# Weight pieces moved from ahead of the expert gathers to behind them, and idle matmuls between the first expert's transposes

## The chip, the cores and the metric

One core of a Trainium2 chip runs the whole program. The metric is the device time of one execution in microseconds; a kernel's time is the median of its executions. Each execution has a state: "slow" when it is over 1.5% above the fastest of the same kernel. A ratio between two kernels is the mean time of one kernel's fast runs over that of the other's fast runs of the same rounds, so it is not quite the ratio of the medians quoted beside it.

## The reference

Attention over 8 batches of 8 heads (576 x 64, block-causal in blocks of 64), then a mixture of 8 experts with the expert of each row given. Cut to the core:

```python
attn_out = _attn_ref(q, k, v)                       # 8 x 8 x 576 x 64
x = attn_out.transpose(0, 2, 1, 3).reshape(4608, 512)
for e in range(8):                                  # w1[e]: 512 x 1024, w2[e]: 1024 x 512
    mask = domain_id == e
    h = np.maximum(x[mask] @ w1[e], 0.0)
    out[mask] = h @ w2[e]
```

## The kernel before

Attention is worked off in 32 pairs of heads. TensorE computes, ScalarE takes the exps, VectorE scales, and each batch's rows x are stored to a buffer in DRAM (`x_rows`). After the last pair GpSimd gathers the rows of each expert from there, five blocks of 128 rows, by an indirect DMA. TensorE transposes a block, runs a first product (relu on ScalarE) and a second product, and GpSimd scatters the result.

The weights of experts 0 to 3 are fetched during the last twelve pairs, in 32 pieces (8 an expert), by the same GpSimd queue that later gathers. `loads(p)` runs once a step:

```python
        if p == 4 * B - 12:
            cast_v(fn, B - 1)
            for e in range(4):
                wts.extend(load_expert(e))          # 8 pieces an expert
        if p >= 4 * B - 12:                         # 13 steps, p = 20 .. 32
            for f in wts[:2]:
                f()
            del wts[:2]
```

So 26 pieces go out ahead of the first gather and 6 behind the first ten. After attention:

```python
    ps = aps.tile([128, 2, 512], F32, name="ps", tag="ps", bufs=2)
    for i in range(36):                             # idle matmuls
        nc.tensor.matmul(out=ps[:, i % 2], lhsT=identh[:], rhs=w1s[0][:, 0, 0:512], ...)
    # ... cut ...
    def gather(tok):
        g = msb.tile([128, NB, DM], F16, name="xg", tag="xg", bufs=3)
        for blk in range(NB):
            nc.gpsimd.indirect_dma_start(out=g[:, blk, :], out_offset=None, in_=xd,
                in_offset=bass.IndirectOffsetOnAxis(ap=tok[:, 1, blk : blk + 1], axis=0), ...)
        return g
    # ... cut ...
    xgs = {e: gather(tok_of(e)) for e in range(2)}
    for f in wts:                                   # the pieces that are left
        f()
    for e in range(E):
        if e + 2 < E:
            xgs[e + 2] = gather(tok_of(e + 2))      # behind those pieces
        # ... first product of e; the second one transposes the rows of e + 1 between its blocks
```

Expert 2's rows are first touched when expert 1's second product begins.

## Time and profile before

| | us |
|---|---|
| time of the kernel before, median of 3 (range) | 333.39 (332.84 to 333.70) |
| the profiled execution | 325.94 (span 323.5, clock 0.950) |
| attention's end (last x) in it | 145.5 |
| first gather / first transposes / first product of expert 0 | 152.7 / 155.9 / 159.5 |
| second product of expert 0 / 1 / 2 starts | 172.5 / 190.9 / 209.3 |

The lines of the page are in the prediction.

### The profile page before, as it was taken

The numbers are of one execution on the slowest core, as the hardware profiler recorded it, in microseconds if no ns is written. First come the engines' busy times: TensorE is split into PE (matmuls) and PEld (weight loads), VectorE is DVE, ScalarE is ACT, GpSimd is POOL, SyncE is SP. The second block draws the span as 40 slices with busy tenths as digits, with TensorE's granted clock in tenths as the row PEclk, the third lists the DMA queues.
The fourth block names the chain that finished last, engine by engine and source line by source line (L and its number), as shares of the span: only waits on it lengthen the run. The fifth ranks groups of instructions, "written<-read, shape, count | busy, mean of one in ns | idle before, by whom it ended". The sixth has DMA issues, their size and how long they took to land. (4 is left out here: it accounts for less than half of the span.)

```text
span 323.5 us, 8592 instructions
## 1 busy us (share of the span) xinstructions
PE 272.4 (84%) x3658; PEld 176.6 (55%) x3658; DVE 154.0 (48%) x298; ACT 146.6 (45%) x208; POOL 205.4 (63%) x274
## 2 busy tenths in 40 slices
PE   2588697978877999777599999999999999999930
PEld 1366565746655766553255665756566565756510
DVE  2868789799857887740103514041322405042220
ACT  5558575758757988750053240605133150604200
POOL 8668989998894833301786648777777876133230
PEclk9999899879979999999589999999999999999995
DMA  7999799998998599995359327979799896112030
GB/s 159 201 220 193 161 267 188 247 211 187 228 200 199 130 208 232 212 235 137 97 126 225 140 83 145 242 187 227 217 198 228 172 229 207 49 65 81 33 118 0
DMA packets 36472, 55.68 MB, mean 172 GB/s; under 512 B 9838, under 2 KB 22638, under 8 KB 36432
## 3 DMA queue, kind: packets, MB, share of 16 engines
q0 software_dynamic: 26128, 49.17, 70.7%
q1 hardware_dynamic: 9776, 5.81, 6.6%
q8 instruction: 30, 0.49, 0.6%
q10 hardware_dynamic: 528, 0.13, 0.2%
q14 instruction: 10, 0.08, 0.1%
HBM read 67.15 MB, written 15.20 MB: 255 GB/s over the span
## 5 line engine op out<-in xcount | busy, mean ns | idle before, releaser
L352 ACT ACTIVATE A<-ps 128x1024 f16<-128x1024 f32 (+1 forms) x96 | 83.2, 883 | 41.0 <-PE ps L347 27.5
L565 ACT ACTIVATE hT<-ph 128x640 f16<-128x640 f32 (+1 forms) x72 | 46.4, 645 | 113.6 <-PE ph L559 94.6
L583 POOL DMA_INDIRECT out_dram<-osb,tok x40 | 40.6, 1014 | 45.5 <-DVE osb L582 35.6
L540 DVE COPY xT<-pt 128x512 f16<-128x512 f16 x40 | 16.9, 425 | 103.2 <-PE pt L537 103.2
L559 PE MATMUL ph<-xT,w1h 128*128 128x320 f16 x384 | 56.4, 307 | 1.1 <-DVE xT L540 1.1
L527 POOL DMA_INDIRECT xg<-x_rows,tok x40 | 40.6, 1015 | 26.0 <-PE ps L515 14.1
L576 PE MATMUL po<-w2h,hT 128*128 128x512 f16 x240 | 56.7, 379 | 0.0
L78 POOL DMA_DIRECT2D vst<-in_v_dram x56 | 42.8, 787 | 14.0 <-DMA kh<-in_k_dram 5.9
L559 PEld LDWEIGHTS <-w1h 128*128 128x128 f16 x384 | 38.5, 100 | 18.9 <-issue 1.4
L339 DVE COPY QK<-PT 128x576 f16<-128x576 f16 x64 | 45.5, 750 | 3.3 <-PE PT L335 3.1
L576 PEld LDWEIGHTS <-hT 128*128 128x128 f16 x320 | 29.9, 98 | 29.3
L347 PE MATMUL ps<-QK 64*128 64x512 f16 (+3 forms) x256 | 37.2, 328 | 5.0 <-issue 2.3
L403 PE MATMUL po<-vS,A 128*128 128x65 f16 x640 | 36.9, 200 | 4.0 <-issue 4.0
L582 DVE COPY osb<-po 128x512 f32<-128x512 f32 x40 | 27.4, 684 | 18.8 <-PE po L576 18.8
L398 PE MATMUL po<-VE,ATE 128*128 128x130 f16 x160 | 33.0, 232 | 3.9 <-DVE x L420 3.1
L403 PEld LDWEIGHTS <-A 128*128 128x128 f16 x640 | 32.1, 102 | 6.6 <-issue 6.5
L420 DVE TENSOR_TENSOR x<-po,rc 128x768 f16<-128x768 f32 x32 | 30.6, 958 | 1.1
L335 PE MATMUL PT<-identh,kh 64*64 64x64 f16 x576 | 16.8, 201 | 8.1 <-DVE inv L234 3.0
L398 PEld LDWEIGHTS <-ATE 128*128 128x128 f16 x160 | 16.0, 100 | 11.9 <-issue 9.7
L537 PE MATMUL pt<-identh,xg 128*128 128x128 f16 x160 | 15.9, 225 | 5.1 <-issue 3.9
L335 PE MATMUL PT<-identh,qh 64*64 64x64 f16 x576 | 16.6, 203 | 4.3 <-DVE QK L339 3.3
L335 PEld LDWEIGHTS <-qh 64*64 64x64 f16 x576 | 13.5, 116 | 12.3 <-issue 10.0
(88 smaller groups left out, 271.8 us busy)
## 6 DMA issues: line engine op xcount, KB each, us to landing
vst<-in_v_dram POOLq DMA_DIRECT2D x63, 128.0 KB, 6.9
w1h<-in_moe_w_dram POOLq DMA_DIRECT2D x24, 256.0 KB, 7.1
w2h<-in_moe_w_dram POOLq DMA_DIRECT2D x24, 256.0 KB, 10.4
vst<-in_moe_w_dram POOLq DMA_DIRECT2D x16, 256.0 KB, 7.4
qh<-in_q_dram POOLq DMA_DIRECT2D x14, 288.0 KB, 6.6
kh<-in_k_dram POOLq DMA_DIRECT2D x14, 288.0 KB, 9.4
x_rows<-x SPq DMA_DIRECT2D x7, 512.0 KB, 10.6
vst<-in_v_dram SPq DMA_DIRECT2D x4, 256.0 KB, 5.6
```

Of the source, the lines that this page charges most:

```text
L78: eng.dma_start(out=vst[b % 3][:, 0:4, n], in_=v[b, n, 0:512, :].rearrange("(c p) d -> p c d", p=128))
L335: nc.tensor.transpose(out=PT[h, j], in_=src[h, hp, 64 * j : 64 * j + 64], identity=identh[h, h])
L339: nc.vector.tensor_copy(out=QK[:, s].rearrange("p (n j) -> p n j", j=9), in_=PT[:].rearrange("p j n -> p n j"))
L347: nc.tensor.matmul(out=o[:, i], lhsT=QK[h, 1, 128 * c : 128 * c + 128], rhs=QK[h, 0, 64 + 128 * c : S], start=True, stop=True)
L352: nc.scalar.activation(out=o, in_=i, func=AF.Exp, scale=0.125)
L398: nc.tensor.matmul(out=o[:, 1:131], lhsT=st["AE"][:, 128 * m : 128 * m + 128], rhs=VE[b % 2][:, m, hp, 1:131], start=True, stop=(m == 0))
L403: nc.tensor.matmul(out=o[:, 1 + 65 * i : 66 + 65 * i], lhsT=at_block(st, i, c, m), rhs=vS[b % 3][:, c, hp, 1 + 65 * i : 66 + 65 * i], star ...
L527: nc.gpsimd.indirect_dma_start(out=g[:, blk, :], out_offset=None, in_=xd, in_offset=bass.IndirectOffsetOnAxis(ap=tok[:, 1, blk : blk + 1], ...
L559: nc.tensor.matmul(out=ph[:, i, 0:hw], lhsT=w1_cols(w1h, dc, fc), rhs=xT[:, dc, hw * i : hw * i + hw], start=(dc == 0), stop=(dc == 3))
L565: nc.scalar.activation(out=hT[:, fc].rearrange("p (i n) -> p i n", i=2)[:, i0:i1], in_=ph[:, i0:i1, 0:hw], func=AF.Relu)
L576: nc.tensor.matmul(out=po[:], lhsT=hT[:, fc, 128 * blk : 128 * blk + 128], rhs=w2h[:, fc, :], start=(fc == 0), stop=(fc == 7))
L583: nc.gpsimd.indirect_dma_start(out=dst[blk], out_offset=bass.IndirectOffsetOnAxis(ap=tok[:, 0, blk : blk + 1], axis=0), in_=osb[:], in_off ...
```

## The change

The intent is to leave the DMA engines to the last stores of x, so that the gathers start sooner, and to keep TensorE's clock up while the first blocks arrive (it was 0.66 from 152.00 to 159.46 us in the profile before). Ten pieces go out ahead of the gathers (one in each of ten steps) and 22 behind the first ten gathers; the 36 idle matmuls write another buffer; five more follow each of expert 0's first two transposed blocks.

```diff
-        if p >= 4 * B - 12:
-            for f in wts[:2]:
+        if 4 * B - 12 <= p < 4 * B - 2:
+            for f in wts[:1]:
                 f()
-            del wts[:2]
+            del wts[:1]
...
-    ps = aps.tile([128, 2, 512], F32, name="ps", tag="ps", bufs=2)
-    for i in range(36):
-        nc.tensor.matmul(out=ps[:, i % 2], lhsT=identh[:], rhs=w1s[0][:, 0, 0:512],
-                         start=True, stop=True)
+    def warm(t, n):
+        for i in range(n):
+            nc.tensor.matmul(out=t[:], lhsT=identh[:], rhs=w1s[0][:, 0, 0:512],
+                             start=True, stop=True)
+
+    warm(aps.tile([128, 512], F32, name="PT", tag="PT", bufs=2), 36)
...
                     transpose_block(xgs[0], xT, blk)
+                    if blk < 2:
+                        warm(mps.tile([128, 512], F32, name="po", tag="po", bufs=2), 5)
```

## The prediction

> **What bounds the kernel now.** I read the page first (busy slices, clock, DMA), then the busy table cut at the borders of the stages, then the timelines of GpSimd and TensorE around the seam between attention and the experts, and last the landing times of the gathers. The chain that ended last holds only the final scatter and is no help.
>
> ```profile
> PEclk9999899879979999999589999999999999999995
> DMA  7999799998998599995359327979799896112030
> ```
>
> DMA is full through the late attention steps, nearly empty for a few slices at the seam, and busy again in the experts. The clock has one deep dip, at the seam. By stage (columns: us, busy us of PE, PEld, DVE, ACT, POOL with counts, clock, DMA share, GB/s):
>
> ```profile
> 107.81:144.02 36.21, 30.84 (x777) 22.60 (x774) 25.70 (x43) 29.45 (x42) 13.85 (x27) 1.00 1.08 217
> 144.02:152.00 7.98, 7.98 (x43) 3.48 (x39) 1.19 (x2) 0.00 (x0) 0.00 (x0) 1.00 0.83 183
> 152.00:159.46 7.46, 1.81 (x13) 1.14 (x13) 1.27 (x3) 0.00 (x0) 5.25 (x6) 0.66 0.25 70
> 159.46:172.21 12.75, 12.12 (x71) 7.45 (x71) 0.76 (x2) 6.22 (x15) 10.62 (x14) 0.80 0.63 132
> 172.21:190.86 18.65, 18.65 (x128) 11.47 (x126) 6.59 (x20) 5.71 (x9) 12.63 (x13) 1.00 0.55 164
> 190.86:310.20 119.34, 119.34 (x786) 71.62 (x784) 33.99 (x64) 34.50 (x49) 72.30 (x87) 1.00 0.67 160
> ```
>
> From 172.21 on TensorE never idles: whatever moves the start of that stretch moves the end by as much, as long as no new wait opens in it. The seam is the only weak place: 152.00 to 159.46 holds 1.81 us of PE work, and 159.46 to 172.21 runs at clock 0.80.
>
> ```profile
> 114.91 0.54 POOL L120 DMA_DIRECT2D w1h<-in_moe_w_dram  x1 [2.82 <-DMA w1h<-in_moe_w_dram]
> 116.15 0.53 POOL L120 DMA_DIRECT2D w1h<-in_moe_w_dram  x1 [0.70 <-DMA w1h<-in_moe_w_dram]
> ...
> 123.79 0.53 POOL L123 DMA_DIRECT2D w2h<-in_moe_w_dram  x1 [0.84 <-DMA w2h<-in_moe_w_dram]
> ...
> 152.69 1.10 POOL L527 DMA_INDIRECT xg<-x_rows,tok  x1 [14.11 <-PE ps L515]
> ...
> 165.56 1.18 POOL L120 DMA_DIRECT2D vst<-in_moe_w_dram  x2
> 166.68 2.18 POOL L123 DMA_DIRECT2D vst<-in_moe_w_dram  x4
> 169.16 1.07 POOL L527 DMA_INDIRECT xg<-x_rows,tok  x1 [0.30 <-issue]
> ```
>
> GpSimd's timeline. Eight weight pieces are in flight at most; each further one waits for the piece eight before it. So the issue times show the rate: 114.91 to 123.79 is seven pieces, 1.27 us each. The first gather (152.69) is put down to the idle matmuls, but in the built program it waits for the last attention matmul and for the stores of x_rows; the idle matmuls come after the counter value it asks for. In the completion records of the trace the last store lands at 151.74, so that store is the gate, and the gather follows 0.95 us later.
>
> ```profile
> 144.07 7.93 PE L515 MATMUL ps<-w1h,identh 128*128 128x512 f16 x36
> ...
> 145.53 0.41 ACTq L436 DMA_DIRECT2D x_rows<-x  x1
> ...
> 155.88 0.59 PE L537 MATMUL pt<-identh,xg 128*128 128x128 f16 x4 [3.88 <-issue]
> ...
> 159.46 7.14 PE L559 MATMUL ph<-xT,w1h 128*128 128x320 f16 x32 [0.52 <-DVE xT L540]
> ...
> 190.91 0.39 PE L537 MATMUL pt<-identh,xg 128*128 128x128 f16 x4
> ```
>
> The timeline of all engines: the last store, issued at 145.53, takes 6.2 us because weight pieces share the DMA engines with it. The last line is the first touch of expert 2's gathered rows (xg), at the start of the second matrix product of expert 1.
>
> ```profile
> DMA to landing us min/median/max: 2.7/3.6/7.8
> ```
>
> The gathers' landing times. The 7.8 is the gather issued at 169.16, right behind six pieces: it lands at 176.95, after the last piece (176.61), and the next four at 0.3 to 1.0 us steps.
>
> [...] A piece reads 128x1024 fp32, 524 KB; in 1.27 us that is 413 GB/s[...]. [...] Here it was 0.5 from 154.33 to 164.57[...], and came back 5.1 us after the dense matmuls began at 159.46.
>
> **The change part by part.** First, pieces. There are 32 (four experts of eight). Before, 26 are issued ahead of the first gather and 6 after the tenth. Now 10 are ahead and 22 after it. "A step" paces nothing on the chip: these loads go to fresh buffers, so GpSimd issues ten as fast as eight in flight allow, and they land by about 127 (the tenth landed at 126.88 before). Attention is not touched: it is held by ScalarE's exps, 29.45 of 36.21 us busy, and by PE at 30.84.
>
> The stores of x_rows are then alone. The store issued at 106.62 and 107.11, which had no weights beside it, landed 3.7 us after its second issue, at 576 rows. The last two stores, about the same number of rows each, should be done at about 148.3, so the first gather starts at 148.3 + 0.95 = 149.3, 3.4 us sooner. Its block lands 2.9 us later as now (152.69 to 155.58), 152.2, just as the 36 idle matmuls end (152.0). Moving them from ps to PT takes off a wait for the last exps but nothing visible: they started 0.05 us behind attention's last matmul.
>
> Second, the idle matmuls between transposes. Blocks land 1.3 us apart; four transposes take about 0.4 us, so five matmuls of 0.216 us (7.93/36 gives 0.22) nearly fill the gap and keep the clock. Warm, the third block is transposed by 155.8, its copy and handover of 0.5 us lead to 156.3, the first half of expert 0's first product costs 32 x 0.134 = 4.3 us instead of 7.1, the two further transposes 1.2 us, the second half 4.6 us: 166.4, where the kernel before is at 172.46. This part with the earlier gather is worth 6.0 us at this point.
>
> Third, what is paid. TensorE goes on: second product 9.75 us (172.46 to 182.21), expert 1's first product 8.7 us: 166.4 + 18.5 = 184.9 when it wants expert 2's rows. Their gather stands behind the 22 pieces in GpSimd's order and in the ring. Ten gathers take 12.87 us of issue (152.69 to 165.56), so the first piece goes out at 162.2. The first piece after the gathers landed 4.28 us after its issue (169.84), now 166.5; 21 more at 1.27 us make 193.2. The rows follow 0.34 us behind (as 176.95 behind 176.61), and TensorE starts 0.27 us later (155.58 to 155.85): 193.8, against 190.91 before. So the lead of 6.0 us becomes a wait of 8.9 us and a lag of 2.9 us.
>
> In a wait that long the clock surely falls. Dense work after it is slow for about as long as before, 5.1 us, and half of that is lost: 2.6 us. Sum: -6.0 + 8.9 + 2.6 = +5.5 us, 338.9 us. The pieces of expert 1 (needed from 176.1, landing from 166.5 to 172.9) and of expert 2 (by 183.1) make nobody wait. Later GpSimd runs some 9 us behind at first, but the gather of expert 4 landed 13 us before its use and expert 4's weights over 20 us, so I see no second wait; nor room to win anything back on a TensorE that is busy throughout.
>
> **The rivals.** (a) The intent comes true: rows of expert 2 are in time, and the 6 us are kept: 327 to 328. For it: the same bytes are moved, and DMA stood at 0.25 to 0.63 between 152 and 172. Against it: 16 more pieces are 20.3 us, and the old gather of expert 2 had only 190.91 - 176.95 = 14.0 us to spare; the 3.4 us of earlier start don't make up the rest. (b) The wait opens but the seam's clock matters little and DMA is a little faster than I count (1.25 us a piece, stores done at 147): wait ends at 192, cold loss 1.7: 336. (c) Stores end later[...]: gather at 150.5, cold loss 3.4: 341. (d) The filler matmuls themselves delay a cold TensorE: at half clock five take 2.2 us in a gap of 0.7 us. It costs up to 3 us at the seam, but disappears in the later wait, as does any gain there. The end depends on the DMA chain alone.
>
> **Range and chances.** The sum is the start of the gather (148.3 to 150.5), the rate of pieces (1.25 to 1.30, times 21 is 1 us) and the cold loss (1.7 to 3.4). Together 335.5 to 342.0. Two per cent slower is 340.06, inside the upper part: 0.28. Two per cent faster is 326.7, beyond even (a): 0.03. Within: 0.69.
>
> **What would show it.** Right: first gather near 149; clock 1.0 through 152 to 166; a PE gap of 7 to 10 us ahead of the transposes of expert 2's rows (released by the DMA of xg), with a clock of 0.5 after it; DMA full from 165 to 193. Wrong: no such gap, or gathers landing ahead of pieces issued before them, or pieces quicker than 1.2 us; then (a). If the gather still starts near 152, the stores were not slowed by the weights.

"Here it was 0.5 from 154.33 to 164.57" speaks of TensorE's clock. That the clock would fall in the later wait too, and that work behind it would again be slow for 5.1 us, was my estimate from this one dip; the range of 1.7 to 3.4 us for the cold loss was assumed.

## The result, and the profile after

The changed kernel took 347.02 us (median of 4, 342.77 to 348.16) beside 333.54 us (median of 4) for the kernel before; the ratio of fast runs is 1.0324, 95% interval 1.0232 to 1.0415. It is slower, and by more than the predicted range allowed. The profiled execution took 348.07 us and is a slow one; its readings are checked below against fast runs.

The clock and DMA rows of the changed kernel's page (40 slices each):

```profile
PEclk9999868787999999999899986999999999999985
DMA  8999899989981990223799947959899595202020
```

DMA, which was full up to about 150 us before, now stands at 0 to 0.3 in slices 16 to 19 (about 130 to 164 us) and is full in slices 21 to 23 (173 to 199 us): the pieces have moved there. The clock's deep dip (slices 20 and 21 before) is gone; there is a slight one left in slice 20 and a new one in slices 24 and 25, 199 to 216 us. By stage, cut at the changed kernel's own borders (columns as in the prediction: us, busy us and count of PE, PEld, DVE, ACT, POOL, then clock, DMA share, GB/s):

```profile
159.86:175.68 15.82, 12.02 (x72) 7.37 (x72) 0.85 (x2) 6.37 (x15) 11.31 (x17) 0.89 0.69 142
175.68:194.29 18.61, 18.61 (x126) 11.21 (x123) 6.69 (x20) 5.43 (x9) 8.92 (x14) 1.00 1.12 209
194.29:198.69 4.40, 0.00 (x1) 0.00 (x1) 0.00 (x0) 0.70 (x1) 3.26 (x4) 1.00 1.00 282
198.69:226.00 27.31, 22.65 (x125) 12.52 (x126) 5.11 (x10) 4.93 (x7) 21.05 (x26) 0.81 0.76 178
```

TensorE is busy without a gap from 175.68 to 194.29, does nothing for 4.40 us while DMA runs full, and then needs 27.31 us for work that took 18.4 before. The next lines are TensorE's timeline in that last stretch (the brackets: idle time before, and what ended it):

```profile
198.69 0.52 PE L539 MATMUL pt<-identh,xg 128*128 128x128 f16 x4 [4.40 <-DMA xg<-x_rows,tok]
...
206.23 0.39 PE L539 MATMUL pt<-identh,xg 128*128 128x128 f16 x4
210.98 3.57 PE L578 MATMUL po<-w2h,hT 128*128 128x512 f16 x8 [4.36 <-issue]
```

The first line is the predicted wait for expert 2's rows. GpSimd's timeline says why they are late: the last piece (`vst`) is issued and, only then, the gather.

```profile
188.51 0.53 POOL L123 DMA_DIRECT2D vst<-in_moe_w_dram  x1 [0.69 <-DMA w2h<-in_moe_w_dram]
189.74 1.06 POOL L529 DMA_INDIRECT xg<-x_rows,tok  x1 [0.70 <-DMA vst<-in_moe_w_dram]
```

The third line of TensorE's timeline above was not predicted. VectorE's timeline has its counterpart:

```profile
209.90 0.42 DVE L542 COPY xT<-pt 128x512 f16<-128x512 f16 x1 [6.12 <-remote]
...
214.20 0.42 DVE L542 COPY xT<-pt 128x512 f16<-128x512 f16 x1 [3.28 <-remote]
```

The transposes that these copies wait for end by 204.67 and 206.62 on TensorE; the copies start 5.23 and, counting from the time when VectorE was free, 3.28 us late. TensorE then runs out of buffers, stands still for 4.36 us, and its clock falls a second time (0.5 from 209.07 to 215.90). I call this a late handover: the producer has ended, the consumer is free, and yet it starts late. The trace's semaphore records place the delay: the count that the two copies wait for rises at 209.88 and 214.18, 0.02 us ahead of them, and not when the transposes end. So it is in 107 of the 108 late handovers of the eight profiles that have any (the count rises at most 0.06 us ahead of the consumer). In the records the count comes late, and the consumer follows it at once. In expert 0's first product the same thing happens between TensorE and ScalarE. First TensorE's lines, then ScalarE's:

```profile
162.20 0.70 PE L561 MATMUL ph<-xT,w1h 128*128 128x320 f16 x4 [0.23 <-ACT hT L567]
163.63 0.70 PE L561 MATMUL ph<-xT,w1h 128*128 128x320 f16 x4 [0.72 <-issue]
165.06 0.70 PE L561 MATMUL ph<-xT,w1h 128*128 128x320 f16 x4 [0.73 <-issue]
```

```profile
161.71 0.44 ACT L567 ACTIVATE hT<-ph 128x320 f16<-128x320 f32 x1 [0.50 <-PE ph L561]
163.14 0.44 ACT L567 ACTIVATE hT<-ph 128x320 f16<-128x320 f32 x1 [0.99 <-PE ph L561]
```

Each group of four matmuls takes 0.70 us and the next begins 1.43 us after it began, because ScalarE begins to empty each of the two buffers about 1.0 us late. The clock is 1.00 there; it falls to 0.5 from 168.11 to 171.52, right after. These gaps have no line of their own in the page: they are found only by subtracting the producer's end from the consumer's start.

### The profile page after: what moved, and what is told of

Its sections match the earlier page's. It is cut to its first block, busy times and chain, and to the rows that moved or that the text cites.

```text
span 346.3 us, 8611 instructions
## 1 busy us (share of the span) xinstructions
PE 280.6 (81%) x3668; PEld 179.6 (52%) x3668; DVE 158.9 (46%) x298; ACT 146.7 (42%) x208; POOL 205.2 (59%) x274
## 5 line engine op out<-in xcount | busy, mean ns | idle before, releaser
L578 PE MATMUL po<-w2h,hT 128*128 128x512 f16 x240 | 60.3, 396 | 8.0 <-issue 4.4
L561 PE MATMUL ph<-xT,w1h 128*128 128x320 f16 x384 | 55.6, 302 | 4.3 <-issue 2.7
L578 PEld LDWEIGHTS <-hT 128*128 128x128 f16 x320 | 30.9, 100 | 42.0 <-issue 14.3
L561 PEld LDWEIGHTS <-w1h 128*128 128x128 f16 x384 | 37.7, 99 | 21.7 <-issue 5.5
L347 PE MATMUL ps<-QK 64*128 64x512 f16 (+3 forms) x256 | 38.0, 335 | 3.8 <-ACT A L352 1.1
L584 DVE COPY osb<-po 128x512 f32<-128x512 f32 x40 | 27.3, 684 | 19.4 <-PE po L578 19.4
L335 PE MATMUL PT<-identh,kh 64*64 64x64 f16 x576 | 17.5, 207 | 9.7 <-DVE inv L232 3.5
L114 POOL CAST vS<-vst 128x1024 f16<-128x1024 f32 (+1 forms) x21 | 19.3, 977 | 6.1 <-DVE QK L339 6.1
L335 PEld LDWEIGHTS <-kh 64*64 64x64 f16 x576 | 15.4, 122 | 11.2 <-issue 9.0
```

The lines of the kernel that those rows point to most:

```text
L335: nc.tensor.transpose(out=PT[h, j], in_=src[h, hp, 64 * j : 64 * j + 64], identity=identh[h, h])
L347: nc.tensor.matmul(out=o[:, i], lhsT=QK[h, 1, 128 * c : 128 * c + 128], rhs=QK[h, 0, 64 + 128 * c : S], start=True, stop=True)
L561: nc.tensor.matmul(out=ph[:, i, 0:hw], lhsT=w1_cols(w1h, dc, fc), rhs=xT[:, dc, hw * i : hw * i + hw], start=(dc == 0), stop=(dc == 3))
L578: nc.tensor.matmul(out=po[:], lhsT=hT[:, fc, 128 * blk : 128 * blk + 128], rhs=w2h[:, fc, :], start=(fc == 0), stop=(fc == 7))
```

## The experiments

Eighteen runs were made in five batches; those of a batch were made on one chip with runs of the kernel before between them. The batches are of two kinds, which the kernel before shows best:

| batch | kernel before, median us (runs) | late handovers over 0.4 us in the profiles |
|---|---|---|
| the first result | 333.54 (4) | changed kernel 12; the profile of before, 325.94 us, none |
| 1: r1_before, r1_after, r1_pieces, r1_after_g3 | 333.09 (23) | in every profile (10 in r1_before, 12 to 19 in the others) |
| 2: r2_filler, r2_plain, r2_after_spread, r2_before_spread | 324.34 (39) | none |
| 3: r3_after, r3_plain, r3_p18, r3_g3 | 333.03 (7) | in all but r3_plain |
| 4: r4_before_plain, r4_plain, r4_pl01, r4_pl23 | 325.11 (7) | none |
| 5: r5_after, r5_pl23 | 324.40 (7) | none |

I say "late batch" for the first kind and "clean batch" for the other. Batches 2 and 3 report the same chip number, 6, so it doesn't tell the kinds apart.

### Batch 1: what does the loss consist of?

r1_before and r1_after are the two kernels unaltered.

> The kernel before, unchanged, run again. The profile on hand of it is of a run of 325.9 us, 7.6 us under the median of the timed runs (333.5), so it may not be the usual state. If the missing time lies in attention (theory A: the length of attention varies by itself), this profile ends attention near 148 to 152 instead of 144.2 and the experts take as long as before from there. If it lies at the seam or in the experts (theory S), attention ends near 144 and some wait of 4 to 7 us shows after it that the first profile lacks. Time 333 to 334.

> The changed kernel, unchanged, run again: 343 to 348 us. Queue theory Q: TensorE stands still before the transposes of expert 2's rows for 4 to 9 us, released by the DMA of xg, with the clock at 0.5 for 3 to 7 us after it. If the gap is there in each profile but its size doesn't cover the 13 us between the medians, something else is lost besides; theory L says that it is lost in expert 0's first product, which ran in lockstep with ScalarE (1.43 us a block of four matmuls) although the clock was full.

r1_before took 332.53 us (1.0013), r1_after 343.97 us (339.84 to 347.68; ratio 1.0282, 1.0132 to 1.0433). The wait for expert 2's rows in r1_after is 5.51 us, and the handovers at expert 2's transposes are up to 4.64 us late. The kernel before has ten late handovers of 0.59 to 2.15 us here, where its first profile had none.

r1_pieces keeps the pieces as the change has them and takes the idle matmuls back:

```diff
-                    if blk < 2:
-                        warm(mps.tile([128, 512], F32, name="po", tag="po", bufs=2), 5)
# and the 36 idle matmuls write ps again, as before
```

> The first part of the change alone: ten pieces before the gathers, the rest after, idle matmuls as before. Theory Q: nearly all the loss is here, 342 to 347 us, the fillers matter less than 2 us. If the fillers or the move of the idle matmuls to PT did the harm (theory F), this is within 2 us of the kernel before, or faster (328 to 335).

346.21 us (338.42 to 348.43), no ratio as three of four runs were slow. The wait is there (6.33 us), and a handover 5.33 us late. Counted from attention's end its profile takes 195.0 us and that of r1_after 194.4 (both slow runs). So, as far as these profiles go, the loss belongs to the pieces; the matmuls between the transposes neither make nor cure it.

r1_after_g3 issues expert 2's gather ahead of the 22 pieces:

```diff
-    xgs = {e: gather(tok_of(e)) for e in range(2)}
+    xgs = {e: gather(tok_of(e)) for e in range(3)}
...
-        if e + 2 < E:
+        if e and e + 2 < E:
```

> The changed kernel with the gather of expert 2 issued straight after those of experts 0 and 1, ahead of the 22 pieces; the same transfers, another order. Theory Q: the wait before expert 2's transposes is gone, and so is the slow clock after it: 6 to 12 us less than the changed kernel, 332 to 338 us. The pieces then start 6.5 us later; expert 1's second product needs six of them by about 180, they land by 180: a small wait may open there. If the loss lies elsewhere, the time stays at 342 or more.

341.73 us (1.031, 1.0209 to 1.0412). The wait is gone: of the idle time before its transposes the profile has only this left, the short pause behind the idle matmuls.

```profile
  PE PT L515: 0.8, 1
```

And yet the time, expected at 332 to 338 us, is no better by fast runs (1.031 beside 1.0282). The hole has moved to expert 0's first product, where ScalarE's handovers come late during the longer row of gathers: with its transposes that product takes 22.1 us. This was the miss that opened the second question: in this batch, taking the predicted wait away is not enough.

### Batch 2: the matmuls alone, the gathers made plain, the gathers spread

r2_filler is the kernel before with the idle matmuls of the change and none of its pieces.

> The second part of the change alone: the idle matmuls in PT and the five after each of the first two transposed blocks, with 26 pieces ahead of the gathers as before. If the fillers keep the clock, expert 0's first product starts at full clock here too. Theory L/N (handovers from TensorE come late while gathers are issued, and most so at full clock) expects that the first half shows blocks of 1.4 us instead of 0.55 and gains under 2 us: 331 to 334 us. Theory K (the clock was all that was lacking at the seam) expects 3 to 5 us gained: 328 to 330.

324.89 us, ratio 1.0005 (0.9973 to 1.0037): nothing. The gather still comes at 152.4 here, after the 36 matmuls have ended, and the clock falls before the new ones begin: the four transposes ahead of them take 0.58 us in place of 0.39. The stretch at clock 0.5 is shorter with them, 3.41 us (10.24 in the first profile of the kernel before), but two sets of five cost 2.34 and 1.49 us, beside 1.24 at full clock in r5_after; counted from attention's end the first product starts 1.3 us later and expert 0's second one 0.8 us sooner. That is the prediction's rival (d). The 3 to 5 us of theory K did not come.

r2_plain replaces the gather of the changed kernel by a read of the same size without indices, wrong result:

```diff
-            nc.gpsimd.indirect_dma_start(
-                out=g[:, blk, :], out_offset=None, in_=xd,
-                in_offset=bass.IndirectOffsetOnAxis(
-                    ap=tok[:, 1, blk : blk + 1], axis=0),
-                bounds_check=N - 1, oob_is_err=False)
+            nc.gpsimd.dma_start(out=g[:, blk, :], in_=xd[128 * blk : 128 * blk + 128, :])
```

> The changed kernel with every gather replaced by a plain GpSimd load of 128 consecutive rows of the same tensor (the result is wrong on purpose); order, bytes and ring are the same. Theory N (it is the indirect gathers, issued back to back for 6 us and more, that delay the handovers): no handover over 0.4 us late, expert 0's first half in 4.5 us, and expert 1's second product 10 us plus its cold clock; together 8 to 12 us less than the changed kernel. Theory Q alone: the wait for expert 2's rows stays, and the rest too, 340 or more.

322.87 us, with three of four runs slow and so no ratio. No handover is late; but none is late in the rest of this batch either, so it told nothing about the gathers.

r2_after_spread and r2_before_spread issue one gather behind each scatter in place of five in a row (`gat` is handed to the second product, which calls `gather_block(*gat, blk)` after each scatter).

> The changed kernel with the gathers of experts 2 to 7 spread: one block after each scatter of the expert two before, instead of five in a row ahead of them. Theory N: the late handovers of experts 1 to 7 are gone (1.4 to 5 us each), the wait for expert 2's rows remains or is some us longer since they now stand behind scatters too: 336 to 341 us. If bursts don't matter: no gain, 342 to 348.

> The kernel before with the same spreading. Theory N: its own late handovers (r1_before had ten, 0.6 to 2.3 us) go away: 326 to 330 us against 333. If bursts don't matter: 332 to 334. A new wait may open if a block's gather lands after its transposes ask for it.

333.29 us (1.0298, 1.0223 to 1.0373) and 326.48 us (1.0087, 1.0050 to 1.0124). Spreading doesn't pay in this clean batch (in a late one it was not tried): in the changed kernel expert 2's gather now also stands behind scatters, and the wait before its transposes is 10.14 us. What this batch gave without being asked is a clean reading of the seam: from attention's end to expert 0's second product r2_after_spread takes 21.6 us, the kernel before 27.0.

### Batch 3: fewer pieces behind, plain gathers, in a late batch

> The changed kernel once more, unaltered. Theory Q (the wait for expert 2's rows behind 22 weight pieces, and the cold clock after it, make the loss; the gain at the seam is real): on a chip where the kernel before takes about 324 us, the wait before expert 2's transposes is 8 to 9 us, expert 0 up to its second product gains some 5 us, and the time is 1.0 to 2.5% above the kernel before (328 to 332 us). Theory N (semaphore signals from TensorE that arrive 1 to 5 us late after bursts of indirect gathers, on some chips alone, make most of the loss): on a chip where the kernel before takes about 333 us there are at least four handovers over 1 us late, expert 0's first half goes in blocks of about 1.4 us, the wait is 4 to 6.5 us, and the time is 343 to 347 us.

> The changed kernel with every indirect gather replaced by a plain read of the same size (wrong result on purpose). Theory N: if the indirect gathers are what makes the late handovers, then on a chip where the changed kernel shows them this one shows none over 0.4 us, and takes 10 us or more less than the changed kernel (333 us or less). Theory Q alone: the transfers and their order in the queue are the same, so the wait for expert 2's rows and the late handovers stay and the time is within 3 us of the changed kernel. On a chip without late handovers it is 320 to 325 us, as it was before (there expert 2's rows came in time).

> The changed kernel with 18 weight pieces instead of 10 ahead of the first gathers (two a step in nine steps), so that 14 instead of 22 stand before expert 2's gather. Theory Q: 8 pieces at 1.27 us are 10 us less of queue, so the wait before expert 2's transposes (5 to 10 us) is gone or under 1 us; the first gather still lands at the attention's end. Chip without late handovers: 317 to 321 us, about 1 to 2% faster than the kernel before. Chip with them (theory N): the wait is gone but handovers up to 5 us late remain, and the time is 333 to 340 us, not faster than the kernel before.

> The changed kernel with expert 2's gather issued right after those of experts 0 and 1, ahead of the 22 pieces. Theory Q: no wait before expert 2's transposes, the seam's gain kept: 317 to 321 us on a chip where the kernel before takes 324. Theory N: on a chip where it takes 333, fifteen indirect gathers in one burst give handovers 1 to 5 us late in expert 0, and the time is 340 to 343 us as in the first run of this kernel.

r3_p18 puts 18 pieces ahead of the gathers, r3_g3 is r1_after_g3 once more:

```diff
-        if 4 * B - 12 <= p < 4 * B - 2:
-            for f in wts[:1]:
+        if 4 * B - 12 <= p < 4 * B - 3:
+            for f in wts[:2]:
```

The kernel before took 333.03 us, r3_after 342.64 (1.0292, 1.0217 to 1.0366), r3_p18 342.65 (1.0236, 1.0155 to 1.0318), r3_g3 343.57 (no ratio). r3_plain took 322.76 us, ratio 0.9688 (0.9621 to 0.9755), 20 us less than the changed kernel beside it by the medians. It has no late handover at all, though its scatters are still indirect. Its stages of expert 0's first product and of experts 1 to 2:

```profile
151.90:162.80 10.90, 10.16 (x72) 6.66 (x72) 0.76 (x2) 6.45 (x15) 6.04 (x12) 1.00 1.06 194
...
183.00:201.40 18.40, 18.40 (x124) 11.29 (x125) 5.21 (x10) 4.93 (x7) 15.97 (x23) 1.00 0.82 211
```

10.90 and 18.40 us, where r3_after, a fast run, takes 13.20 and 26.70:

```profile
157.90:171.10 13.20, 10.46 (x72) 6.65 (x72) 0.76 (x2) 6.31 (x15) 10.29 (x15) 1.00 0.67 137
...
196.30:223.00 26.70, 22.05 (x124) 12.41 (x125) 5.21 (x10) 4.93 (x7) 21.01 (x25) 0.86 0.75 179
```

So in this late batch no handover is late once the gathers are not indirect. Not all of the gain is handovers. The spans of the two profiles differ by 24.7 us (341.0 and 316.3): 5.5 are a shorter attention (see below), 5.0 the wait for expert 2's rows (6.6 and 1.6), which shrinks as a plain read also costs GpSimd less (ten took 5.3 us in r4_pl01, ten indirect gathers 12.9), and with that wait goes the cold clock behind it, 2.6 us in the clean run of batch 5. That leaves some 11 to 12 us for the handovers, which is an estimate.

r3_p18 missed its expectation of 333 to 340 us, and shows how: it has no wait for expert 2's rows, but ScalarE gets the blocks of expert 1's first product late. That product begins at 185.9, as the gathers of expert 2 end (186.6), and those of expert 3 run beside it from 193.4 to 199.7:

```profile
193.10 0.70 ACT L567 ACTIVATE hT<-ph 128x640 f16<-128x640 f32 x1 [5.20 <-remote]
198.10 0.70 ACT L567 ACTIVATE hT<-ph 128x640 f16<-128x640 f32 x1 [4.29 <-remote]
```

That product takes 22.4 us in place of 8.7. The two versions that should have beaten both kernels beat neither here; in a clean batch they were not run.

### Batch 4: which gathers, and what the change is worth without them

> The kernel before with every indirect gather replaced by a plain read of the same size (wrong result on purpose). Theory N (the indirect gathers make the late handovers): on a chip where the kernel before takes about 333 us its late handovers are gone and it takes 323 to 326 us, 2 to 3% less; on a chip where it takes 324 us nothing changes (322 to 325). If instead the time is that of the kernel before where that is 333, the gathers cost nothing there and theory N falls.

> The changed kernel with every gather plain, once more, beside the kernel before with every gather plain. If the change does in TensorE's order what the prediction said and only the gathers spoilt it, this one takes 319 to 323 us and is 2 to 5 us shorter than the kernel before with plain gathers, with expert 0 up to its second product some 5 us shorter. Rival: the gain comes from the plain reads' shorter issue on GpSimd alone; then the two are equal within 1 us.

> The changed kernel with the gathers of experts 0 and 1 alone plain. Theory N, on a chip where the changed kernel takes 343: expert 0's first half takes 4.3 to 5.5 us in place of 8 to 10 (no blocks of 1.43 us); the pieces are issued some 7 us earlier, so the wait for expert 2's rows is gone or under 1 us; handovers over 1 us late stay where the gathers of experts 2 and 3 run; 331 to 337 us. If the blocks of 1.43 us stay, those gathers don't make them.

> The changed kernel with the gathers of experts 2 and 3 alone plain. Theory N, on a chip where the changed kernel takes 343: expert 0's first half stays at 8 to 10 us, the wait for expert 2's rows is 2 to 4 us shorter, and the handovers of 2 to 5 us at expert 2's transposes are gone, so from the start of expert 1's second product to expert 2's takes 18 to 22 us in place of 27; 331 to 336 us. If the late handovers at expert 2's transposes stay, the gathers of expert 3 that run beside them don't make them.

r4_before_plain and r4_plain are the two kernels with all gathers plain, r4_pl01 and r4_pl23 the changed kernel with those of experts 0 and 1, or 2 and 3, plain:

```diff
-    def gather(tok):
+    def gather(tok, plain=False):
         ...
+            if plain:
+                nc.gpsimd.dma_start(out=g[:, blk, :], in_=xd[128 * blk : 128 * blk + 128, :])
+                continue
```

The batch was a clean one (before 325.11 us), so the late half of the expectations could not be tested. Times: 319.29 (0.9824, 0.9775 to 0.9872), 321.51 (0.9862, 0.9787 to 0.9938), 325.14 (0.9897, 0.9794 to 1.0000), 329.24 (1.0154, 1.0094 to 1.0214). Two things follow.

First, the wait depends on how long GpSimd needs for the first ten gathers. Indirect ones take it 12.9 us, 1.0 each and 0.3 between two, as the prediction counted; plain ones took 5.3 us (154.3 to 159.6 in r4_pl01), so all 22 pieces and expert 2's gather move up by about 7.5 us. The idle time before the transposes is, in r4_pl01 (under 1 us was expected) and then in r4_pl23, where only the later gathers are plain:

```profile
  DMA xg<-x_rows,tok: 1.7, 1
```

```profile
  DMA xg<-x_rows: 8.8, 1
```

Second, an expectation that failed: with plain gathers in both, the change should have won 2 to 5 us, and it won nothing (319.29 against 321.51). The windows from attention's end to expert 0's first product, then expert 0's second product and expert 1's first, in r4_before_plain and then in r4_plain:

```profile
145.30:154.20 8.90, 7.72 (x43) 3.58 (x42) 1.24 (x4) 0.00 (x0) 4.46 (x9) 1.00 0.62 172
...
165.20:183.60 18.40, 18.40 (x125) 11.25 (x124) 6.60 (x20) 5.42 (x9) 7.78 (x10) 1.00 0.35 127
```

```profile
145.60:155.70 10.10, 9.53 (x54) 4.56 (x52) 1.27 (x3) 0.00 (x0) 6.45 (x13) 1.00 0.54 157
...
166.60:186.10 19.50, 18.60 (x126) 11.18 (x123) 6.60 (x20) 6.15 (x10) 8.68 (x15) 1.00 1.11 227
```

In the unchanged kernel with plain gathers the blocks arrive before the clock has fallen (it is 1.00 throughout), so there is nothing to save at the seam, and this kernel is 1.8% faster than with indirect gathers where no change was expected in a clean batch; the ten extra matmuls cost 1.2 us net, and the wait for expert 2's rows still costs 0.9.

### Batch 5: the changed kernel in a clean batch

> The changed kernel, unaltered. If the kernel before takes about 325 us here (no late handovers): the wait before expert 2's transposes is 8 to 10 us, the stretch from expert 1's second product to expert 2's takes 20 to 21 us (the predicted 18.4 plus 2.6), expert 0 from the attention's end to its second product 21 to 23 us, no handover is over 0.4 us late, and the time is 328 to 331 us, 1.0 to 2.0% over the kernel before. If the kernel before takes about 333 us here: 342 to 347 us, with handovers up to 5 us late, as in the other runs of it.

> The changed kernel with the gathers of experts 2 and 3 alone plain. Without late handovers: within 2 us of the changed kernel (329 us as in its first run). With them: expert 0's first half still takes 8 to 10 us, and if the gathers of experts 2 and 3 make the late handovers at expert 2's transposes, those are gone and the stretch from expert 1's second product to expert 2's takes 19 to 22 us in place of 27, for 332 to 337 us; if they stay, other traffic makes them and the time is 340 us or more.

r5_after took 331.33 us (328.38 to 337.51) beside 324.40: ratio 1.0157, interval 1.0067 to 1.0248. r5_pl23 took 329.92 us (1.0171, 1.0070 to 1.0273). No handover is late in either. The expectation for r5_after held but for the time, which is 0.3 us over. The stages of r5_after, which answer to those of the changed kernel's first profile above:

```profile
155.40:166.34 10.94, 10.21 (x73) 6.70 (x73) 0.76 (x2) 6.50 (x15) 9.41 (x14) 1.00 0.58 125
166.34:184.89 18.55, 18.55 (x125) 11.15 (x123) 6.59 (x20) 5.40 (x9) 7.32 (x15) 1.00 1.12 208
184.89:193.70 8.81, 0.02 (x2) 0.02 (x2) 0.00 (x0) 0.70 (x1) 6.75 (x7) 0.71 1.06 248
193.70:214.70 21.00, 21.00 (x125) 12.23 (x126) 5.21 (x10) 4.93 (x7) 16.78 (x21) 0.88 0.63 155
```

And from its timeline, the first half of expert 0's first product in one run of 32 matmuls, and the wait:

```profile
155.36 5.06 PE L561 MATMUL ph<-xT,w1h 128*128 128x320 f16 x32 [0.52 <-DVE xT L542]
...
193.68 0.61 PE L539 MATMUL pt<-identh,xg 128*128 128x128 f16 x4 [8.79 <-DMA xg<-x_rows,tok]
```

Whether the gathers of experts 2 and 3 are those that delay the handovers at expert 2's transposes stays open: r4_pl23 and r5_pl23 both fell in clean batches.

### The four kernels side by side

Times in us from attention's end (the end of the last x), each from one profile and good to about 0.1. "Clean" is the first profile of before and r5_after, "late" is r1_before and r3_after; all four are fast runs. (The first profile of the changed kernel, late and slow, is in the last column.)

| start of | before, clean | before, late | after, clean | after, late | after, first |
|---|---|---|---|---|---|
| first gather | 7.2 | 7.7 | 4.0 | 3.8 | 4.0 |
| first product of expert 0 | 14.0 | 14.3 | 10.8 | 10.6 | 10.8 |
| second product of expert 0 | 27.0 | 27.4 | 21.7 | 23.8 | 26.6 |
| second product of expert 1 | 45.4 | 48.8 | 49.1 | 49.0 | 49.6 |
| second product of expert 2 | 63.8 | 67.2 | 70.1 | 75.7 | 76.9 |
| end of span | 178.0 | 185.1 | 184.9 | 193.7 | 197.2 |

Clean, the change loses 6.9 us after attention; late, 8.6 (12.1 in the first profile). Attention itself ends between 141.8 and 151.5 us in the profiles. By pair 20 the spread is there already (105.6 to 114.8), and up to that pair the two programs do the same; from pair 20 on all profiles take 34.5 to 37.4 us. So the order of the pieces does not stretch attention. The spread goes with the clock in those first pairs, and it is what sets the slow profiles apart: the eight slow ones end attention at 149.1 to 151.5 us, with 23.9 to 30.7 us at half clock ahead of the first weight piece; the twelve fast ones end it at 141.8 to 147.3, with 13.7 to 23.9. All five profiles of kernels with the old order are fast ones, eight of the 15 with fewer pieces ahead are slow; whether that is chance stays open, and it is part of why the medians lie further apart than the ratios: 13.5 us by the recorded medians, 10.8 by the fast runs.

## Why the prediction was right or wrong

**The wait for expert 2's rows: right; that it fits to the tenth is luck.** Predicted: TensorE wants the rows at 184.9, the last piece lands at 193.2, TensorE goes on at 193.8. In r5_after TensorE wants them at 184.89, the last piece lands at 193.25, the first block at 193.64, and TensorE goes on at 193.68. But the first gather came 0.7 us sooner than predicted (148.58), since attention ended 0.9 us sooner than in the profile that the working used, and from it to the last piece it took 44.7 us and not 43.9. Counted from attention's end the lag is 3.7 us and not 2.9. The reading of the queue as the bound holds: rival (a), that the six microseconds are kept, is out. One number on the way was read wrongly and cost nothing: the 413 GB/s count the fp32 source of a piece, while the profile counts 256 KB a piece and 208 GB/s in the stretch of pieces. That pieces can go no faster was not shown. The rate held all the same, 27.5 us for 21 pieces (26.7 predicted).

**The earlier first gather: right.** 4.0 us after attention's end in place of 7.2, so 3.2 sooner; predicted were 3.4. The working has a gap here: 3.7 us after an issue at 145.53 would be 149.2 and not 148.3. The measured landing, 3.05 us after attention's end (147.63 in r5_after), lay nearer to the number used (2.8) than to the 3.7.

**The seam's gain of 6.0 us: right where handovers are in time, and without weight.** Clean it is 5.3; the first half costs 5.06 us in place of 4.3 (the second half of the kernel before, at full clock, already showed 4.95). Late, the gain is 3.6 between the two late columns and 0.8 for the first profile. But rival (d) had the point that matters: whatever happens at the seam disappears in the wait. The four profiles of the changed kernel (r1_after: 25.4 and 49.6) differ by 4.9 us at expert 0's second product and by 0.6 at expert 1's. The end depends there on the DMA chain alone.

**The cold loss, "half of that is lost: 2.6 us": right clean, wrong in the late runs, of which the recorded result is made; this is the term that failed.** From expert 1's second product to expert 2's takes 18.4 us before. Clean it takes 21.0 after the change, 2.6 more: in r5_after the clock was 0.5 from 188.6 to about 198.9, and TensorE worked in the last 5.2 us of that (5.1 estimated). Late it takes 26.7 and 27.3, so the term measured 8.3 to 8.9 us. In the first profile the difference is the late copies at 209.90 and 214.20, the 4.36 us in which TensorE stands still, and the second fall of the clock, which begins in that stop (0.5 from 209.07 to 215.90). That stop is a second wait, which the prediction did not see. After it the change costs nothing more: from expert 2's second product to the end the late column takes 118.0 us against 117.9 in the late kernel before (114.8 and 114.2 clean). In the late columns the loss of 8.6 us is thus this term with its 8.3; the lag ahead of it is only 0.2 (49.0 and 48.8) in place of 2.9, as late handovers in expert 1's first product had already cost the kernel before 2.9 us (11.6 in place of 8.7).

**The step behind it: the base.** The sum of +5.5 us was worked out from an execution of 325.94 us and added to a time of 333.39. Clean, that sum holds: the ratio of fast runs, 1.0157, makes +5.1 (+6.9 by the medians, which hold slow runs). But the timed runs were late ones, to judge by the kernel before in them. The 7.5 us between the profile and the times were in plain sight. They are about the size of what late handovers cost the kernel before: r1_before takes 7.1 us longer after attention than the clean profile. Adding a difference from one kind of run to a time of the other takes for granted that the change meets them as the old order did. It doesn't: the ratios are 1.0282 to 1.0324 in late batches, some 9 to 11 us, against 1.0157 clean.

**What is shown and what is not.** Shown, by one profile: in a late batch, making the gathers plain removes every late handover (r3_plain beside r3_after). A plain read also keeps GpSimd for a shorter time (5.3 us for ten, against 12.9), so what about the indirect gathers does it isn't separated. Shown as a coincidence in time: of the 108 late handovers 75 wait while a row of gathers is being issued and 31 more begin to wait within 4.2 us of the end of one; such rows fill about 51 of the 133 us from the first gather to the last in r3_after. The longest delays move with them: in expert 0 for r1_after_g3, in expert 1's first product for r3_p18, at expert 2's transposes for the change. Not shown: what in the hardware delays a signal, or why some batches are free of it.

One thing separates the two kinds of profile without exception: records. Clean profiles hold 4,264 to 4,272 records of DMA completions (the first profile of before 4,267). Those with late handovers hold 3,298 to 3,361 (the first profile of the changed kernel 3,308), complete up to the first gathers and with gaps from there on; r3_plain holds 3,942 and has no late handover. The "remote" in place of a releaser in the lines above fits such a gap. Fewer records and late signals go together in eight profiles, and r3_plain, 8% short of 4,272, has no late signal: whether the one has to do with the other is not shown. Every execution here was given with its span and clock, so each was recorded in some way, and no run can tell whether the recording itself takes a part of the time.

## What to carry to other kernels

In GpSimd's queue the transfers landed here in the order of issue (in r5_after the last piece at 193.25, the gather behind it at 193.64), and the pieces moved away from one critical place stood in front of the next user, who waited 8.79 us. So count a queue's work up to each later deadline, with its issue costs (ten gathers 12.9 us), before crediting the gain. And before adding a predicted difference to a measured time, check that the profile it came from is of the same kind as the timed runs; if they differ by more than the effect that you predict, find out why first. A consumer that starts long after its producer ended, while free (up to 5.33 us here), is a cause of its own: look for it by subtraction, because no line of the profile names it.
